# Score and product passes on 64x128 tiles beside PV sums on 64x32 tiles in a fused attention and gated MLP kernel

## Chip, cores and metric

The kernel runs on one core of a Trainium2 chip, as one program. The metric is the device time of one execution in microseconds (us). TensorE (PE in the profile) multiplies matrices on an array of 128 rows by 128 columns, which can be addressed in tiles: a form such as `64*32` in the profile means a tile of 64 rows (of the contraction) and 32 columns (of the output's partitions). ScalarE is ACT, VectorE DVE, GpSimd POOL, and SyncE (SP) issues most DMAs.

## The reference

What is computed, with x of shape 1 x 2048 x 448 in bf16, 16 heads of 28 columns and a hidden layer of 1792:

```
xn  = layernorm(x)
q, k, v = split(xn @ wqkv)                       # 16 heads, 28 columns each
p   = softmax(q @ k^T * 28**-0.5)                # 2048 x 2048 for each head
s   = (p @ v, heads side by side) @ wo
g   = silu(gelu(xn @ w1 + b1) @ w2 + b2)
out = x + s * g
```

## The kernel before

The heads are taken in 4 groups of 4 (`G`), the queries in 4 chunks of 512 (`C`): 16 blocks. A block has 64 score tiles `m`: 16 key tiles of 128 keys times 4 heads, each 128 keys x 512 queries in one bank of the PSUM ring of 8 banks (`ring`). Scores stand with the keys on the partitions. ScalarE takes the exponential of two banks (at times three) at once into `P` (L1790); some score tiles ("late" ones) go instead through a bit trick on VectorE (`p_apass`, L2075) into spare pieces of other buffers (`x_sb`, `w2`, `kT`, `vaug`, `h` and so on), which is why the inputs of L2341 have so many names in the profile. The PV sums (`t_pv`, L2341) multiply these with `vaug` or `vs`: 28 value columns of a head, a column for the denominator and three of zeros, so 32 columns a head; the 4 heads of a group go into the 4 column strips of one accumulator bank. Between these run the products: queries, keys and values of the later groups (L136, L1517), the hidden layer (L136 with `w1`), the second layer (L136 with `w2`), the output projection (L136 with `wo`). VectorE takes most of their banks out again. In the tables these lines carry the names that the profile gives (`w<-h` for a product of `h` with `w2`, for instance).

The order of all of this is made before anything runs: the class `_Kernel` is a list scheduler in Python. Processes (`p_scores`, `p_exps`, `p_pv`, `p_f1` and others) yield tasks with an engine, reads, writes and a planned duration; `run` picks the next task by its earliest start and its priority and puts it at the end of its engine's queue, with the semaphore waits that `deps` finds. The durations are constants in the text (`STEP` = 0.216 for a pass); how many matmuls a task issues does not enter.

TensorE works in one of four modes. `full` uses the whole array, `col` uses tiles of 128*32 for products and PV sums, `row` uses tiles of 32*128 for up to four scores of different heads (`t_score`, L1711). In the first 51 us and the last 38 us these take turns. In between, for most of blocks 0 to 14 (`HB0`, `HB1`), the mode is `half`: the array's rows are two halves, 0 to 63 and 64 to 127, and each pass uses one half `h`. A score tile (`t_half`, L1734) takes the two heads of its half, with the queries in `qp` laid out so that the rows of the other head are zero. A product splits its contraction of 128 into two halves, which one after another add into the same bank (`product`, lines 514 to 527). A PV pass adds the 64 keys of its half for four tiles (`t_pv` with `h`). A half pass, before, is four matmuls on four tiles of 64*32, at `tile_position` (64h, 0), (64h, 32), (64h, 64), (64h, 96): for scores and products these are four strips of the same output, for PV sums the four heads. Planner and TensorE can so keep both halves busy with passes of any kind. The planner counts a price (`SWITCH` = 0.1) where the mode changes, and none inside `half`; between halves it waits where the same bank is written by the other half (lines 249 to 252).

Filler passes (`filler`, `p_busy`) multiply zeros into the accumulator where TensorE would be idle for long; there are few. `p_qn` (L1448) writes four strips for four chunks and keeps its own tiles.

## Time and profile before

| what | value |
|---|---|
| median of 2 runs | 430.15 us (429.64 to 430.67) |
| the profiled execution | 428.93 us, its span 426.7 us |
| TensorE matmuls | 408.6 us busy (96%), 12,221 instructions |
| TensorE weight loads | 208.1 us busy (49%), 12,221 instructions |
| ScalarE | 403.8 us busy (95%), 435 instructions |
| VectorE | 331.0 us busy (78%), 568 instructions |
| GpSimd | 224.8 us busy (53%), 250 instructions |
| mean granted TensorE clock | 0.999 |
| the costliest matmul groups | L1734 64\*32 scores 200.7 us (x3460); L136 `w<-h` 99.0 (x1736); L2341 `P`, `vaug` 93.3 (x971); L136 `xnT`, `w` 88.4 (x1664) |

How to read it: busy time is the union of an engine's instructions. Matmuls overlap one another, and each ends some 0.17 us after it has taken in its last column, so a busy TensorE is not one at its peak; the time from the start of one matmul to the start of the next on the same tile is the better measure. In a timeline row stand the start in us, the length of the row, the engine, the line, the operation, what is written and read, the tile (rows\*columns), the shape of the moving operand, the count, and in brackets the idle time before and what ended it. In a row of the windows stand the window, its length, and then busy time and count for matmuls, weight loads, VectorE, ScalarE and GpSimd (for one line: matmuls and weight loads alone), the granted clock, the DMA share and GB/s. In a row of the waits stand who waited, for whom, the total, the number of times and the longest.

### The profile page before, as it was taken

Reading aid. Unit: us, or ns where it says so; the run is one execution under the profiler, and the core shown is the slowest. Engines: PE = TensorE matmul, PEld = TensorE weight load, DVE = VectorE, ACT = ScalarE, POOL = GpSimd, SP = SyncE. Lnnn points to the kernel's source line nnn. Section 1 sums busy time; section 2 is a strip of 40 time slices with the busy share of each in tenths; the row PEclk is TensorE's granted clock in tenths of the full one; section 3 lists DMA queues with packets and bytes.
Section 4 is the critical chain, followed back from the end, with each engine's and each line's share of the span. In section 5 each row is a group of like instructions: output and inputs, shape, how many; then the busy total and the mean of one; then the engine's idle time right before and its main releaser. Section 6 shows DMA issues by size and latency. Waiting matters only on the chain.

```text
span 426.7 us, 27054 instructions
## 1 busy us (share of the span) xinstructions
PE 408.6 (96%) x12221; PEld 208.1 (49%) x12221; DVE 331.0 (78%) x568; ACT 403.8 (95%) x435; POOL 224.8 (53%) x250
## 2 busy tenths in 40 slices
PE   6999999989999999999999999999999999999996
PEld 5443245554444444444445645445655555544563
DVE  8958987946888779996876426448698979778985
ACT  6999999989999999999999899889999999999794
POOL 7496376526376535348444723517735435765040
PEclk9999999999999999999999999999999999999999
DMA  8702201011001000101141330501010101011056
GB/s 251 274 3 47 33 4 42 21 28 36 22 4 38 17 24 17 39 7 28 25 148 42 59 73 7 113 4 32 17 30 17 30 18 29 6 47 29 3 102 144
DMA packets 21233, 20.41 MB, mean 48 GB/s; under 512 B 9709, under 2 KB 17693, under 8 KB 21086
## 3 DMA queue, kind: packets, MB, share of 16 engines
q1 hardware_dynamic: 18990, 15.10, 12.6%
q0 software_dynamic: 1152, 3.02, 4.2%
q8 instruction: 95, 1.56, 1.5%
q10 hardware_dynamic: 976, 0.57, 0.5%
q14 instruction: 20, 0.16, 0.1%
HBM read 12.54 MB, written 2.88 MB: 36 GB/s over the span
## 4 chain that ended last, share of the span: by engine, by line
PE 86%; ACT 6%; issue 4%; DVE 2%; POOL 1%; ACTq 0%; POOLq 0%; DVEq 0%
PE ring L136 31%; PE ring L1734 25%; PE ring L2341 23%; ACT P L1790 5%; PE ring L1711 3%; PE ring L1517 2%; PE ring L1307 1%; ACT h L1790 1%; POOL x_sb L2142 0%; ACT xnT L1790 0%; PE ring L1238 0%; DVE h L2500 0%; PE ring L1259 0%; DVE h L2477 0%; DVE qT L1294 0%
## 5 line engine op out<-in xcount | busy, mean ns | idle before, releaser
L1790 ACT ACTIVATE P<-ring 128x1024 bf16<-128x1024 f32 (+1 forms) x241 | 236.1, 1112 | 7.1 <-PE ring L1734 2.0
L1734 PE MATMUL ring<-qp,kT 64*32 64x512 bf16 x3460 | 200.7, 381 | 2.3 <-issue 0.9
L1734 PEld LDWEIGHTS ring<-qp,kT 64*32 64x32 bf16 x3460 | 59.0, 89 | 87.8 <-ACT P L1790 35.2
L136 PE MATMUL ring<-w,h 64*32 64x448 bf16 (+1 forms) x1736 | 99.0, 350 | 0.0
L2341 PE MATMUL ring<-P,vaug 64*32 64x512 bf16 (+3 forms) x971 | 93.3, 361 | 1.1 <-PE ring L1734 0.7
L1790 ACT ACTIVATE h<-ring 128x1024 bf16<-128x1024 f32 (+1 forms) x92 | 88.5, 1135 | 1.8 <-PE ring L1734 0.9
L136 PE MATMUL ring<-xnT,w 64*32 64x512 bf16 x1664 | 88.4, 377 | 1.5 <-issue 1.4
L2075 DVE TENSOR_SCALAR vaug<-ring 128x512 uint16<-128x512 f32 x68 | 45.1, 684 | 14.1 <-PE ring L1734 6.2
L136 PEld LDWEIGHTS ring<-w,h 64*32 64x32 bf16 (+1 forms) x1736 | 41.9, 92 | 16.2 <-issue 1.8
L1790 ACT ACTIVATE xnT<-ring 128x1024 bf16<-128x1024 f32 (+2 forms) x44 | 45.5, 1088 | 1.7 <-PE ring L2341 1.0
L2341 PE MATMUL ring<-h,vaug 64*32 64x512 bf16 (+2 forms) x405 | 44.7, 376 | 0.2
L136 PEld LDWEIGHTS ring<-xnT,w 64*32 64x32 bf16 x1664 | 33.4, 91 | 21.4 <-PE ring L136 3.9
L2448 POOL TENSOR_TENSOR qT<-x_sb,E_sb 128x512 bf16<-128x512 f32 x15 | 17.5, 1165 | 49.6 <-DMA x_sb<-recs 39.7
L2437 POOL TENSOR_TENSOR rc<-rs,mone 128x16 f32<-128x16 bf16 x11 | 32.9, 2988 | 19.3 <-DMA rs<-E_sb 14.5
L2075 DVE TENSOR_SCALAR w<-ring 128x512 uint16<-128x512 f32 x52 | 34.8, 686 | 7.4 <-PE ring L1734 3.5
L2075 DVE TENSOR_SCALAR x_sb<-ring 128x512 uint16<-128x512 f32 x48 | 32.0, 686 | 9.3 <-PE ring L1734 7.6
L2341 PEld LDWEIGHTS ring<-P,vaug 64*32 64x32 bf16 (+1 forms) x971 | 28.0, 92 | 10.9 <-issue 1.6
L136 PE MATMUL ring<-xnT,wq 64*32 64x512 bf16 (+1 forms) x372 | 30.4, 379 | 1.2 <-issue 1.0
L136 PE MATMUL ring<-xnT,wk 64*32 64x512 bf16 (+1 forms) x360 | 28.2, 379 | 0.2 <-ACT P L1790 0.2
L2341 PE MATMUL ring<-x_sb,vs 64*32 64x512 bf16 (+1 forms) x284 | 27.4, 377 | 0.3 <-POOL x_sb L2142 0.3
L2341 PE MATMUL ring<-xnT,vaug 64*32 64x512 bf16 (+2 forms) x208 | 26.8, 341 | 0.4 <-issue 0.4
L1538 DVE TENSOR_SCALAR h<-ring,b1c 128x512 bf16<-128x512 f32 x32 | 23.8, 744 | 2.7 <-PE ring L136 2.0
(251 smaller groups left out, 764.7 us busy)
## 6 DMA issues: line engine op xcount, KB each, us to landing
x_sb<-recs SPq DMA_DIRECT2D x60, 64.0 KB, 2.2
qp<-qT SPq DMA_DIRECT2D x60, 32.0 KB, 2.2
w<-in_B_w_dram SPq DMA_DIRECT2D x1, 1568.0 KB, 8.6
w<-in_B_w_dram SPq DMA_DIRECT2D x1, 1344.0 KB, 8.5
x_sb<-in_A_x_dram SPq DMA_DIRECT2D x2, 448.0 KB, 5.7
out_dram<-in_A_x_dram SPq DMA_DIRECT2D x2, 448.0 KB, 10.5
out_dram<-h POOLq DMA_DIRECT2D x4, 224.0 KB, 5.7
out_dram<-h SPq DMA_DIRECT2D x7, 112.0 KB, 1.7
```

What stands on the lines that cost most here:

```text
L136: ins = eng.matmul(out[q:q + 32, :], w[:, q:q + 32], x, tile_position=(r0, q), start=start, stop=stop, skip_group_check=True)
L1307: yield _Task(PE, lambda eng: eng.matmul(bank[:, 0:256], K.ident[:, :], K.E_sb[:, 0, 0:256], start=True, stop=True), [K.b_id, K.b_pads], [ ...
L1517: ins = eng.matmul(bank[q:q + 32, 0:12 * DH], K.xnT[r0:r0 + n, k, t * 128 + q:t * 128 + q + 32], ap, tile_position=(r0, q), start=start, s ...
L1538: yield _Task(DVE, lambda eng: eng.tensor_scalar(dst, bank, K.b1c[:, ft:ft + 1], None, op0=ALU.add), [tok, K.b_b1c], wr, 0.69, 0.0, 2)
L1711: return eng.matmul(dst, K.kT[32 * j:32 * j + 32, g, t * 128:(t + 1) * 128], K.qT[32 * j:32 * j + 32, g, c * 512 + q0:c * 512 + q0 + nq], ...
L1734: ins = eng.matmul(bank[q:q + 32, col:col + nq], K.kT[sl, g, t * 128 + q:t * 128 + q + 32], K.qp[sl, b % 2, v, q0:q0 + nq], tile_position= ...
L1790: return eng.activation(reg[:, i0:i0 + n, :], src, ACTF.Exp, scale=SM_SCALE)
L2075: yield _Task(DVE, lambda eng: eng.tensor_scalar(K.part(u, k).bitcast(dt.uint16), K.like(u, bank), SM_SCALE * LOG2E * 128.0, (127.0 - EXP_ ...
L2341: return eng.matmul(acc[32 * j:32 * j + 32, q0:q0 + nq], w[sl], ap[sl, col:col + nq] if len(ap.shape) == 2 else ap[sl, col // 128:(col + n ...
L2437: yield _Task(POOL, lambda eng: eng.tensor_tensor(K.rc[:, :], K.rs[:, :], K.mone[:, 0:1].to_broadcast([128, 16]), ALU.pow), [K.b_srs, K.b_ ...
L2448: yield _Task(POOL, lambda eng: eng.tensor_tensor(dst, K.rb, E, ALU.mult), [K.b_rb, tE], [K.b_onT[g][c]], 1.15, 0.05, 1, port=True)
```

## The change

Three places issue the half passes of scores and products: `_mm`, which serves most products, the fillers and the second layer; `f` in `p_v1`, for the values of groups 1 to 3; and `f` in `t_half`, for scores. Each now issues one matmul on a tile of 64*128 at position (64h, 0) in place of the four. Without `h` (modes `col` and others) `_mm` and `p_v1` are as they were. PV sums and `p_qn` keep their tiles of 64*32. The planner's durations and priorities, and so every queue's order and all waits, stay.

```
 def _mm(eng, out, w, x, start, stop, h=None):
     ...
-    for q in range(0, 128, 32):
-        ins = eng.matmul(out[q:q + 32, :], w[:, q:q + 32], x, tile_position=(r0, q), start=start, stop=stop, skip_group_check=True)
+    n = 32 if h is None else 128
+    for q in range(0, 128, n):
+        ins = eng.matmul(out[q:q + n, :], w[:, q:q + n], x, tile_position=(r0, q), start=start, stop=stop, skip_group_check=True)
     return ins

 # p_v1
-            for q in range(0, 128, 32):
-                ins = eng.matmul(bank[q:q + 32, 0:12 * DH], K.xnT[r0:r0 + n, k, t * 128 + q:t * 128 + q + 32], ap, tile_position=(r0, q),
+            w = 32 if h is None else 128
+            for q in range(0, 128, w):
+                ins = eng.matmul(bank[q:q + w, 0:12 * DH], K.xnT[r0:r0 + n, k, t * 128 + q:t * 128 + q + w], ap, tile_position=(r0, q),
                                  start=start, stop=True, skip_group_check=True)

 # t_half
             for t, q0, nq, col in pc:
-                for q in range(0, 128, 32):
-                    ins = eng.matmul(bank[q:q + 32, col:col + nq], K.kT[sl, g, t * 128 + q:t * 128 + q + 32], K.qp[sl, b % 2, v, q0:q0 + nq],
-                                     tile_position=(64 * h, q), start=True, stop=True, skip_group_check=True)
+                ins = eng.matmul(bank[:, col:col + nq], K.kT[sl, g, t * 128:t * 128 + 128], K.qp[sl, b % 2, v, q0:q0 + nq],
+                                 tile_position=(64 * h, 0), start=True, stop=True, skip_group_check=True)
             return ins
```

## The prediction

> **What bounds the kernel now.** I read the page first, its busy shares, its clock row and its chain, then the windows for the stretch that the change touches, then the timeline row by row.

> ```profile
> span 426.7 us, 27054 instructions
> ...
> PE 408.6 (96%) x12221; PEld 208.1 (49%) x12221; DVE 331.0 (78%) x568; ACT 403.8 (95%) x435; POOL 224.8 (53%) x250
> ...
> PEclk9999999999999999999999999999999999999999
> ...
> PE 86%; ACT 6%; issue 4%; DVE 2%; POOL 1%; ACTq 0%; POOLq 0%; DVEq 0%
> ```

> TensorE and ScalarE are both nearly full, at full clock, and 86% of the chain that ended last is matmuls. ScalarE makes the exponentials from the scores; anything that slows TensorE by more than a few per cent makes ScalarE wait, and nothing hides it. The passes in two row halves (tile 64*32) fill one stretch, from the first row of L1734 in that form to the first score row back in 32*128:

> ```profile
> 51.10:389.40 338.30, 329.98 (x10665) 168.80 (x10662) 257.04 (x403) 329.16 (x343) 182.91 (x175) 1.00 0.14 33
> ...
> 51.10:389.40 338.30, 194.34 (x2552) 64.13 (x2552) 1.00 0.14 33
> ...
> L1734 PE MATMUL ring<-qp,kT 64*32 64x512 bf16 x3460 | 200.7, 381 | 2.3 <-issue 0.9 <-ACT P L1790 0.8 <-DVE wq L2075 0.4
> ...
> PEld ring L1734 <- ACT P L1790: 35.2, 123, 1.0
> ```

> The first row is all engines (matmuls, weight loads, VectorE, ScalarE, GpSimd), the second L2341, the PV sums, alone: 2,552 of 10,665 matmuls. A pass is four of them, one per 32 columns. The last row shows the slack there is: score loads wait 35.2 us for exponentials, in 123 places. Inside this stretch the two halves run side by side whatever they compute:

> ```profile
> 108.03 0.39 PE L2341 MATMUL ring<-h,vaug 64*32 64x512 bf16 x4
> 108.06 0.39 PE L1734 MATMUL ring<-qp,kT 64*32 64x512 bf16 x4
> 108.25 0.38 PE L2341 MATMUL ring<-h,vaug 64*32 64x512 bf16 x1
> 108.25 0.38 PE L2341 MATMUL ring<-P,vaug 64*32 64x512 bf16 x3
> 108.28 0.39 PE L136 MATMUL ring<-xnT,wq 64*32 64x512 bf16 x4
> 108.46 0.39 PE L2341 MATMUL ring<-P,vaug 64*32 64x512 bf16 x4
> 108.50 0.39 PE L136 MATMUL ring<-xnT,w 64*32 64x512 bf16 x4
> 108.71 0.40 PE L1734 MATMUL ring<-qp,kT 64*32 64x512 bf16 x8
> ```

> A PV pass in one half starts at 108.03, a score pass in the other 0.03 us later, and so on: three PV passes beside a score and two product passes, six passes in 108.71 - 108.03 = 0.68 us. A half takes a new pass each 0.216 us or so (108.03, 108.25, 108.46). All of them have one shape, so nothing separates them.

> **What a change of shape costs.** The change gives scores and products the shape 64*128 and leaves the PV sums at 64*32. That pair is nowhere in this trace, but other changes of shape are:

> ```profile
> 15.63 0.39 PE L1711 MATMUL ring<-qT,kT 32*128 32x512 bf16 x2 [0.18 <-DVE xnT L1152]
> 15.96 0.39 PE L1307 MATMUL ring<-E_sb,ident 128*128 128x256 bf16 x2
> 16.28 0.62 PE L136 MATMUL ring<-xnT,wk 128*32 128x512 bf16 x8
> ...
> 20.44 0.39 PE L1711 MATMUL ring<-qT,kT 32*128 32x512 bf16 x2
> 20.76 0.61 PE L2341 MATMUL ring<-P,vaug 128*32 128x512 bf16 x8
> 21.31 0.39 PE L1711 MATMUL ring<-qT,kT 32*128 32x512 bf16 x2
> ...
> 52.02 0.41 PE L1734 MATMUL ring<-qp,kT 64*32 64x512 bf16 x8
> 52.36 0.62 PE L2341 MATMUL ring<-h,vaug 128*32 128x512 bf16 x8
> ```

> From 20.44 to 20.76 is 0.32 us where the same shape would have followed after 0.216: 0.10 us is lost. It is the same when only the rows change (52.02: two passes, the second 0.01 later, then 0.33 to 52.36) and when only the columns change (15.96: two matmuls of 256 columns, 0.107 each, so streaming ends at 16.17, and the next starts at 16.28). I did this for all 111 neighbours of different shape in the timeline: none starts less than 0.090 us after the stream before it should have ended, 92 lie between 0.090 and 0.107 (the others waited for something else), the median is 0.099. For 64*32 to 64*128 I take 0.098, with 0.090 and 0.106 as ends; its nearest row is the change of columns alone, at 15.96.

> Does one half's change stop the other half? Two rows near the end say so:

> ```profile
> 393.33 0.75 PE L136 MATMUL ring<-w,h 64*32 64x448 bf16 x12
> ...
> 394.01 0.12 PEld L1711 LDWEIGHTS ring<-qT,kT 32*128 32x128 bf16 x6 [0.37 <-issue]
> 394.01 0.40 PE L1711 MATMUL ring<-qT,kT 32*128 32x256 bf16 x6
> ```

> By the kernel's list the three product passes at 393.33 are all in the lower half (rows 64 to 127), and the first score matmul behind them is head row 1, rows 32 to 63, which nobody uses. It still starts only at 394.01: the third pass starts at 393.33 + 0.75 - 0.36 = 393.72 and streams 0.19 us, to 393.91, and then the usual 0.09 to 0.10 passes; the view names no other releaser ("issue"). So a change waits for both halves. [...]

> **The change, part by part.** Removed: three of four matmuls and loads of each score and product pass. L136, L1517 and L1734 have 8,112 matmuls of shape 64*32, 2,028 passes, so 6,084 go and about 6,137 of 12,221 stay. That gains next to nothing: four matmuls of a pass start 3 ns apart and stream together, and the half is busy 0.216 us either way. Walking the list of passes with one clock for each half, 0.216 us per 512 columns and a few ns of issue, gives 304.4 us for the stretch with four matmuls a pass and 302.7 with one. The stretch took 338.3, so 33.9 us of it are waits for banks and other engines.

> Added: the changes of shape. No pass moves in any queue and no DMA is touched. The stretch holds 642 PV-like passes (2,552 matmuls of L2341, of which 8 are in another shape, and 24 of one small line that keeps 64*32) between 1,994 score, product and filler passes. In the list they fall into 552 runs of PV passes and 556 runs of the others; 488 of the PV runs are a single pass, and 543 of 552 lie in one half alone, so the other half stands idle meanwhile. With three short returns to 128*32 there are 1,111 changes. A run lasts as long as its fuller half, then both drain:

> - PV runs: 632 passes in the fuller halves x 0.2158 = 136.4 us.
> - Score and product runs: 1,295 passes in the fuller halves (831 of 512 columns, 369 of 448, 86 of 336, 9 fillers) = 262.9 us.
> - 1,111 changes x 0.098 = 108.9 us.
> - Stagger of the halves inside runs and the three short returns: 5.6 us.

> Together 513.8 us (504.9 with 0.090 a change, 522.7 with 0.106). The six passes from 108.03 show it small: six runs of one pass, 6 x (0.216 + 0.098) = 1.88 us in place of 0.68.

> Of the 33.9 us of waits most should go: score loads no longer wait for exponentials, since a pair of scores now comes each 1.6 us or so and its exponential takes about 1.1. What is left are turns of one bank from half to half, where TensorE waits for its own pass in the other half; between two such turns there is now a change or two more. The bounds are 0 and 33.9; I take 6, near the lower end, since TensorE takes 1.5 times as long for the same order. Behind each drain stands the rest of TensorE's queue; the first to wait for it is ScalarE for scores, then VectorE for products and late scores, both with time to spare then.

> A weight load of 128 columns in place of 32 could show after a change, where nothing covers it. The drain at 20.44 to 20.76 leads into 32-column loads, the one at 393.33 to 394.01 into 128-column loads, and both are 0.09 to 0.10, so I add nothing; the case is a rival below.

> Sum: the profiled execution took 428.93 us, 2.2 outside its span of 426.7. 428.93 - 338.3 + 513.8 + 6 = 610.4. The median of the runs shown, 430.15, lies 1.2 higher. I say **610 us**.

> **The rivals.**

> - Each half drains by itself, and the other goes on. The list then has 659 changes within a half, and the walk gives 352.9 us. Some to all of the 33.9 us of waits stay, since ScalarE is again close: 428.93 - 338.3 + 352.9 + 17 = 460 (443 to 477). For it: the halves are separate rows. Against: the row at 394.01.
> - Not slower: between 64*32 and 64*128 there is no change at all for the hardware, since the rows stay. One place decides, the start of a PV pass in one half while a score pass streams in the other: if it may start, nothing is added and the walk falls by 1.7, to 427. Against: 15.96 to 16.28, where the columns alone change. With even a zero price but shapes that exclude each other the walk is 405.0, so the time 502.
> - The longer loads show: behind each of the 556 changes into 64*128 a whole load of 92 ns (the row of L1711 below) stands after the drain. 556 x 0.092 = 51: 661. Against: that row is of 128-column loads too, and the drains into them are no longer than others. [...]
> - Two 64*128 passes cannot stream side by side. Then score and product runs take the sum of their halves, 404.7 in place of 259.6 of pure stream, 145 more: 755. Against: four row tiles of 128 columns start together in the last row below, and are done in 0.41 us, as two are in 0.39 at 20.44.

> ```profile
> L1734 PEld LDWEIGHTS ring<-qp,kT 64*32 64x32 bf16 x3460 | 59.0, 89 | 87.8 <-ACT P L1790 35.2 <-ACT h L1790 13.0 <-ACT xnT L1790 5.8
> ...
> L1711 PEld LDWEIGHTS ring<-qT,kT 32*128 32x128 bf16 x287 | 8.4, 92 | 18.1 <-ACT P L1790 5.2 <-issue 4.8 <-ACT h L1790 2.3
> ...
> 31.21 0.41 PE L1711 MATMUL ring<-qT,kT 32*128 32x512 bf16 x4
> ```

> **How the numbers follow.** Drain of both halves at each change: 0.80. Each half by itself: 0.07. No drain: 0.05. Drain at no price but no overlap: 0.03. Longer loads that show: 0.03. No two passes side by side: 0.02. The likeliest case's own range is 428.93 - 338.3 + 504.9 = 595 to 428.93 - 338.3 + 522.7 + 33.9 = 647; I reach a little beyond both ends, 580 to 660, for what the walk leaves out. Only the case without a drain lies within 2% of before, about what a measurement of this kernel can tell: same 0.04, faster 0.01, slower 0.95.

> **What would show it.** Right: about 6,140 matmuls; in the timeline, rows of L2341 and of score lines no longer overlap and start 0.31 us after one another where single; ScalarE's share falls from 95% to about 66% (403.8 of 608) with idle time put down to L1734's successor; clock still full. The stretch of the two halves is near 520 us and the rest of the span, 88 us, as before. Wrong: PV and score rows that start within 0.05 us of one another; then the time is under 480. Or a gap after a change well off 0.10 us: each 0.01 is 11 us.

## The result, and the profile after

The changed kernel takes 640.38 us (638.01 to 642.74, two runs) against 430.15: 1.489 times the time before, interval 1.464 to 1.514. Four further runs gave 638.63 us (636.62 to 641.75) beside 430.01 for the kernel before, ratio 1.486 (1.479 to 1.494). The profiled execution took 642.74 us, its span 640.5.

The page of the kernel after, from its first, second and fourth part, and the ScalarE group of the fifth (busy time, mean ns, then idle time before and what ended it):

```profile
span 640.5 us, 14886 instructions
...
PE 628.9 (98%) x6137; PEld 204.9 (32%) x6137; DVE 335.7 (52%) x568; ACT 428.6 (67%) x435; POOL 223.5 (35%) x250
...
PEclk9999999899999999999999998559996699999999
...
PE 93%; DVE 2%; ACT 2%; issue 1%; DMA 0%; ACTq 0%; DVEq 0%
...
L1791 ACT ACTIVATE P<-ring 128x1024 bf16<-128x1024 f32 (+1 forms) x241 | 247.1, 1053 | 122.8 <-PE ring L1735 99.8
```

Matmuls fell to 6,137, and yet TensorE is 98% busy and 93% of the chain. ScalarE does the same 435 instructions, but at 67% of the span: it now waits 99.8 us for score rows alone in this group. The clock row, all nines before, has three dents.

The timeline of the kernel after, matmuls only, near the same time as the passes quoted before from 108.03 (an earlier place in the order):

```profile
107.76 0.40 PE L2342 MATMUL ring<-h,vaug 64*32 64x512 bf16 x4
108.09 0.31 PE L1519 MATMUL ring<-wv,xnT 64*128 64x336 bf16 x1
108.09 0.39 PE L1735 MATMUL ring<-qp,kT 64*128 64x512 bf16 x1
108.24 0.30 PE L1519 MATMUL ring<-wv,xnT 64*128 64x336 bf16 x1
108.38 0.38 PE L1735 MATMUL ring<-qp,kT 64*128 64x512 bf16 x1
108.69 0.40 PE L2342 MATMUL ring<-w,vaug 64*32 64x512 bf16 x4
109.02 0.31 PE L1519 MATMUL ring<-wv,xnT 64*128 64x336 bf16 x1
```

Two passes on 64\*128 tiles start together at 108.09, one in each half, so these do overlap. The PV pass does not: the four matmuls of L2342 start alone at 108.69, 0.31 us after the score row at 108.38 (0.216 of streaming and 0.09 more), and the next shape starts 0.33 us after that. Between 108.69 and 109.02 one half of the rows does nothing. The six passes quoted before stand at 138.5 to 140.65 here: the score pass joins the scores ahead of it, and the other five start runs of their own, at 139.03, 139.36, 139.67, 140.00 and 140.32, with the next run at 140.65; that is 0.32 us a run. The view of the waits, TensorE's loads, gives such time no releaser ("issue"; total, times, longest):

```profile
PEld ring L2342 <- issue: 140.2, 456, 0.8
...
PEld ring L137 <- issue: 86.8, 348, 0.4
```

Where the clock row dents, the windows of the same execution (window, length, busy time and count of matmuls, loads, VectorE, ScalarE, GpSimd, then granted clock, DMA share, GB/s) are:

```profile
51.00:395.70 344.70, 343.71 (x3011) 107.34 (x3011) 173.53 (x263) 239.51 (x232) 123.13 (x122) 1.00 0.09 23
395.70:429.90 34.20, 34.20 (x170) 7.42 (x166) 9.20 (x14) 12.91 (x13) 4.96 (x3) 0.50 0.03 10
429.90:484.50 54.60, 54.60 (x474) 16.92 (x470) 26.15 (x41) 33.70 (x33) 17.47 (x15) 1.00 0.04 11
484.50:508.40 23.90, 23.90 (x130) 5.99 (x130) 6.88 (x12) 9.05 (x8) 6.18 (x6) 0.50 0.01 1
508.40:604.00 95.60, 95.60 (x846) 29.26 (x847) 46.89 (x75) 59.71 (x59) 31.90 (x31) 1.00 0.07 16
```

Two windows, 58.1 us together, ran at half clock with TensorE busy in all of their length; a third of 3.4 us at 119.3 lies inside the first row, whose mean still rounds to 1.00.

The account: the stretch in halves went from 338.3 to 552.2 us (50.98 to 603.18), what follows it stayed at 37.3, what precedes it at 51. The 552.2 are 513.8 that the walk through the order gave, 5.6 because a change of shape cost 0.103 us in the mean at full clock rather than 0.098 (1,111 changes), 27.6 for the half clock, and 5.2 that is left for waits and all else. (The mean of 0.103 holds 14 changes that waited for something else; without them it is 0.101, and some 2 us move from the second term to the last.) The 27.6 is worked out: 61.4 us were spent at half clock, and the walk gives 33.8 us for the same passes at full clock.

### The profile page after: what moved, and what is told of

Read it like the earlier page. It is cut to its first block, busy times and chain, and to the rows that moved or that the text cites. A ratio compares the mean times of both kernels' runs of the same rounds, so it can differ in the third digit from the quotient of the medians.

```text
span 640.5 us, 14886 instructions
## 1 busy us (share of the span) xinstructions
PE 628.9 (98%) x6137; PEld 204.9 (32%) x6137; DVE 335.7 (52%) x568; ACT 428.6 (67%) x435; POOL 223.5 (35%) x250
## 4 chain that ended last, share of the span: by engine, by line
PE 93%; DVE 2%; ACT 2%; issue 1%; DMA 0%; ACTq 0%; DVEq 0%
PE ring L2342 34%; PE ring L137 34%; PE ring L1735 20%; PE ring L1519 3%; PE ring L1713 2%; ACT P L1791 2%; DMA x_sb<-in_A_x_dram 0%; DVE st L1069 0%; DVE w L2394 0%; DVE h L2501 0%; PE ring L1449 0%; PE ring L1260 0%; DVE h L2480 0%; DVE h L2478 0%; DVE qT L1295 0%
## 5 line engine op out<-in xcount | busy, mean ns | idle before, releaser
L1791 ACT ACTIVATE P<-ring 128x1024 bf16<-128x1024 f32 (+1 forms) x241 | 247.1, 1053 | 122.8 <-PE ring L1735 99.8
L1735 PE MATMUL ring<-qp,kT 64*128 64x512 bf16 x865 | 219.9, 398 | 0.7 <-DVE vaug L2076 0.4
L137 PE MATMUL ring<-w,h 64*128 64x448 bf16 (+1 forms) x476 | 125.5, 381 | 0.0
L2342 PE MATMUL ring<-P,vaug 64*32 64x512 bf16 (+3 forms) x971 | 106.9, 381 | 0.0
L137 PE MATMUL ring<-xnT,w 64*128 64x512 bf16 x416 | 95.2, 380 | 0.1
L1735 PEld LDWEIGHTS ring<-qp,kT 64*128 64x128 bf16 x865 | 50.7, 95 | 70.9 <-issue 43.9
L137 PEld LDWEIGHTS ring<-w,h 64*128 64x128 bf16 (+1 forms) x476 | 35.4, 98 | 60.2 <-issue 46.8
L2342 PE MATMUL ring<-h,vaug 64*32 64x512 bf16 (+2 forms) x405 | 48.5, 384 | 0.1
L2342 PEld LDWEIGHTS ring<-P,vaug 64*32 64x32 bf16 (+1 forms) x971 | 26.7, 91 | 64.1 <-issue 40.9
L137 PEld LDWEIGHTS ring<-xnT,w 64*128 64x128 bf16 x416 | 28.1, 94 | 38.9 <-issue 19.5
L137 PE MATMUL ring<-xnT,wq 64*128 64x512 bf16 (+1 forms) x141 | 31.9, 383 | 0.2 <-DVE w L2076 0.2
L2342 PE MATMUL ring<-xnT,vaug 64*32 64x512 bf16 (+2 forms) x208 | 29.9, 385 | 0.0
L137 PE MATMUL ring<-xnT,wk 128*32 128x512 bf16 (+1 forms) x150 | 29.5, 382 | 0.2 <-ACT P L1791 0.2
L2342 PE MATMUL ring<-x_sb,vs 64*32 64x512 bf16 (+1 forms) x284 | 28.9, 397 | 0.0
```

Of the source, the lines that this page charges most:

```text
L137: ins = eng.matmul(out[q:q + n, :], w[:, q:q + n], x, tile_position=(r0, q), start=start, stop=stop, skip_group_check=True)
L1735: ins = eng.matmul(bank[:, col:col + nq], K.kT[sl, g, t * 128:t * 128 + 128], K.qp[sl, b % 2, v, q0:q0 + nq], tile_position=(64 * h, 0), s ...
L1791: return eng.activation(reg[:, i0:i0 + n, :], src, ACTF.Exp, scale=SM_SCALE)
L2342: return eng.matmul(acc[32 * j:32 * j + 32, q0:q0 + nq], w[sl], ap[sl, col:col + nq] if len(ap.shape) == 2 else ap[sl, col // 128:(col + n ...
```

## The experiments

Theory A: a change between 64\*32 and 64\*128 drains both halves, at about 0.10 us, and while passes of one shape run none of the other can; the time follows the order of shapes. Theory C, the rival: a pass on a 64\*128 tile costs more by itself, so the loss (209 us for 2,028 passes) follows the number of such passes. A third question is the clock.

**after_again** is the kernel after once more, to size the half clock.

> The changed kernel unaltered, in several executions. Theory A: the 28 us by which it is over the forecast are the time at the half clock (61 us of it in the profiled execution, where streaming takes twice as long). Then executions differ in their clock, and the time goes with it: about 0.44 us more per us at half clock, so some 613 us + 0.44 x (time at half clock), 638 to 643 at 0.958 to 0.95. Rival B: the 28 us come from waits or a higher price of a change of shape; then the time does not go with the clock.

Measured: 638.63 us as above, and the profile has its dents at 119 to 143 and 542 to 573: the first begins where the short one did and lasts longer, the other is at a new place. The pairs of granted clock and span, with the first two runs, are 0.950 and 640.5, 0.958 and 635.9, 0.957 and 637.4, 0.960 and 635.8, 0.955 and 639.7, 0.962 and 634.5. Time at half clock is 2 x (1 - clock) x span, so 48 to 64 us; from the last pair to the first, 15.8 us more of it make the span 6.0 longer, about 0.4 us for each. So the loss to the clock is real, near 20 to 28 us in every run, and not tied to one place in the order.

**scores_only** and **products_only** do one part of the change each.

```
 # scores_only: the edit in t_half alone; _mm and p_v1 as before
 # products_only: the edits in _mm and p_v1 alone; t_half as before
```

> Scores on 64x128, products and PV sums on four tiles of 64x32. Theory A (each change of shape drains both halves, 0.103 us): the list has 891 changes, and the walk with two clocks gives 450 us for the stretch of the halves in place of 524; with 84 us outside it and some 8 of waits 540 to 550 us at full clock, up to 20 more where the clock falls. Rival C (each 64x128 pass costs something for itself, its longer load above all): 864 of 1,994 passes have the new shape, so 430 + 0.43 x 210 = 520 us. The two lie close here; products_only tells them apart.

> Products on 64x128, scores and PV sums on four tiles of 64x32. Theory A: fewer passes have the new shape than in the changed kernel, but there are more changes, 1,199 against 1,117, since scores now stand against products; the walk gives 538 us, so about 625 to 632 us at full clock and 640 to 665 with 30 to 60 us at half clock: no faster than the changed kernel. Rival C (a price for each 64x128 pass): 1,130 of 1,994 passes, 430 + 0.57 x 210 = 549 us.

Measured, one run each: scores_only 542.2 us, clock 0.998, 865 passes changed and 891 changes of shape: inside A's 540 to 550, and C's 520 is out. products_only 692.03 us, with 1,163 passes changed and 1,199 changes of shape: slower than the whole change, which C (549) excludes. It is also slower than A's figure, which allowed at most 60 us at half clock. Its windows show why:

```profile
51.00:477.00 426.00, 424.22 (x5706) 132.16 (x5698) 209.12 (x320) 286.02 (x278) 145.31 (x140) 1.00 0.09 21
477.00:613.60 136.60, 136.60 (x994) 27.76 (x990) 36.69 (x58) 44.64 (x42) 23.68 (x23) 0.50 0.03 6
```

136.6 us at half clock; with 0.45 us lost in each (27.6 of 61.4), 61 us, which leaves 631, inside A's 625 to 632 for full clock. A's mechanism holds, and my size for the clock was a miss.

**micro** leaves out the whole of the computation and runs streams of matmuls, with 50 of 128\*128 ahead of each.

```
A  100 passes of 64*128, both halves in turn, 512 columns
B  the same with four of 64*32 a pass
C  60 passes: 64*128 in the upper half, four of 64*32 in the lower, in turn
D  60 passes: the same pair, both in the upper half
E  as C, 100 passes of 128 columns
F  250 of 64*128 in the upper half alone
G  250 of 32*128 in one quarter of the rows alone
H  as D, 200 passes
```

> Not the reference's computation: x is copied out, and TensorE runs streams of matmuls on a part of wqkv, each after 50 matmuls of 128x128. A: 100 passes of 64x128 in both halves in turn. B: the same with four of 64x32. C: 64x128 in the upper half and four of 64x32 in the lower, in turn, 512 columns. D: the same, both in the upper half. E: as C with 128 columns. F: 250 passes of 64x128 in one half, nothing changes. G: 250 of 32x128 in one row tile. H: 200 as D. Theory A (a change drains both halves, about 0.10 us whatever streams): a pass starts 0.108 us after the one before in A and B, 0.31 in C and D, 0.155 in E. Rival D (each half drains by itself): C as A, 0.108 us, and D 0.31. Rival C (long loads show): A slower than B. On the clock: if it is held by how much of the array works (F half, G a quarter, H about a third, all without a gap of over 0.2 us), it falls in G and perhaps in H, not in F; if it is held by TensorE having something to do at all, it stays full in all three.

Measured in its timeline, matmuls only, the streams A, B and the starts of C and D:

```profile
16.92 10.96 PE L32 MATMUL ps<-w 64*128 64x512 bf16 x100
...
38.71 10.99 PE L37 MATMUL ps<-w 64*32 64x512 bf16 x400
...
60.53 0.39 PE L32 MATMUL ps<-w 64*128 64x512 bf16 x1
60.84 0.40 PE L37 MATMUL ps<-w 64*32 64x512 bf16 x4
61.17 0.39 PE L32 MATMUL ps<-w 64*128 64x512 bf16 x1
61.49 0.40 PE L37 MATMUL ps<-w 64*32 64x512 bf16 x4
...
102.16 0.39 PE L32 MATMUL ps<-w 64*128 64x512 bf16 x1
102.48 0.40 PE L37 MATMUL ps<-w 64*32 64x512 bf16 x4
```

One shape throughout costs 0.11 us a pass, wide or four strips alike (10.96 and 10.99 us for 100), so wide passes run side by side and are not dearer. The two shapes in turn cost 0.32 us a pass (60.53, 60.84, 61.17, 61.49), three times as much, though they lie in different rows. D, in the same rows, is 0.32 too (102.16, 102.48), so a change in one half drains the other. E takes 0.16 us a pass for streams of 128 columns, some 0.05 us each: the price of about 0.10 does not hang on the length. The streams C and D agree and set the price.

The clock in the same run, by windows around the stream C, for F, and for G:

```profile
60.50:66.20 5.70, 5.70 (x46) 1.72 (x45) 0.00 (x0) 0.00 (x0) 1.00 0.00 0
66.30:89.30 23.00, 22.87 (x109) 4.52 (x107) 0.00 (x0) 0.00 (x0) 0.50 0.00 1
177.30:231.20 53.90, 53.90 (x251) 23.38 (x250) 0.00 (x0) 0.00 (x0) 1.00 0.00 1
242.20:247.10 4.90, 4.90 (x24) 2.15 (x24) 0.00 (x0) 0.00 (x0) 1.00 0.00 0
247.20:344.00 96.80, 96.80 (x228) 33.22 (x226) 0.00 (x0) 0.00 (x0) 0.50 0.00 0
```

C fell to half clock 5.7 us after its start. F, half of the array without a change, kept full clock for 53.9 us. G, a quarter of the array without any change or pause, fell after 4.9 us and stayed down. D, E and H fell as well, 4.4 to 5.5 us after their start. TensorE was busy all the time; what differs is how much of the array took in columns: 0.50 in F, 0.25 in G, and in C one half at a time for 0.216 of each 0.325 us, so 0.33.

**uniform** takes the other way to one shape: the PV sums in halves become one matmul on a 64\*128 tile too. It leaves out three quarters of these PV sums (the four heads' weights side by side meet the scores of one head only), so its time shows the shapes, with the same passes, order and waits.

```
 # the change, and in t_pv with h, for the first of four heads alone:
+ eng.matmul(acc[:, q0:q0 + nq], w4[sl], <scores>, tile_position=(64 * h, 0), ...)   # w4: vaug or vs of four heads, 128 columns
```

> Every half pass is one matmul of 64x128, PV passes too: of a PV pass's four products only the one of the first head is computed, against the value columns of all four heads, so three quarters of the PV sums are left out. The passes, their order and the time that each streams are as before, and but for six passes nothing changes shape. Theory A (the loss is in the changes of shape): the walk gives 303 us for the stretch in place of 304, so 426 to 431 us, same as before, and the clock stays full, since both halves work. Rival C (64x128 costs something for itself: its load, or two of them not side by side): slower than before, toward 640.

Measured: 421.24 us (420.96 to 421.93) beside 431.31, ratio 0.977 (0.974 to 0.979). With every half pass on a 64\*128 tile nothing of the loss is left, and the clock is 1.0: the wide tile is harmless, mixing is not. It came 5 us below A's 426 to 431: that it beats before by 10 us I had not expected; the last section comes back to it.

**runs30, runs5** and **runs3** keep the order and give the wide tile only to passes that stand in a run of at least 30, 5 or 3 passes without a PV pass; the rest keep four of 64\*32.

```
+LONG = 30        # 5, 3
 # _mm, p_v1, t_half:
+n = 128 if <run of this task has LONG tasks or more> else 32
 for q in range(0, 128, n): ...
```

> Order as before; 64x128 only in score and product passes that stand in a run of 30 or more of them without a PV pass between: 266 passes in 3 runs, the longest in the GELU stage. Theory A: a handful of changes more, the walk 310.2 against 308.8 us, less what 800 fewer matmuls save: 427 to 432 us, same as before. If 64x128 passes themselves were the loss (Rival C), 13% of them would cost some 28 us.

> As the one before, with runs of 5 or more: 1,158 of 1,994 passes at 64x128, but only 243 changes in place of 1,117. Theory A: the walk gives 351 us against 309, of which the 29.5 us of waits in the old order cover a part: 453 to 472 us, clock full. Rival C (by passes): 430 + 0.58 x 210 = 552 us.

> As before, with runs of 3 or more: 1,660 passes at 64x128 and 548 changes. Theory A: the walk gives 411 us, waits mostly covered: 505 to 525 us at full clock. Rival C: 430 + 0.83 x 210 = 604 us.

Measured:

| kernel | passes on 64\*128 (matmuls in the trace) | changes of shape | time |
|---|---|---|---|
| runs30 | 266 | 6, around 3 runs | 425.33 us (beside 428.84), ratio 0.993 (0.991 to 0.996) |
| runs5 | 1,171 | 243 | 448.57 us, one run |
| runs3 | 1,684 | 548 | 506.38 us, one run |
| scores_only | 865 | 891 | 542.2 us, one run |
| the change | 2,028 | 1,111 | 638.63 us |

More passes do not cost more: runs5 and runs3 have more wide passes than scores_only and are faster. C's figures, 552 and 604, are both out. runs5 came 4 us below A's range and runs30 2 us below its own, runs3 inside it. By the 2% that the prediction took for what one measurement can tell, runs30 is the same as the kernel before; over 10 and 13 runs its interval lies 0.4 to 0.9% below it and does not reach 1, so a small gain is likely real. Of the kernels that compute everything it is the fastest.

**priced** lets the planner know: a change of shape inside `half` costs `SWITCH`, as a change of mode does, and drains. **priced32** runs that new order on the old tiles of 64\*32, so that no change of shape is left in it.

```
+ if t.mode != self.pe_mode or t.mode == "half" and t.shape != self.pe_shape:   # shape=1 for PV tasks
 # priced: with the change; priced32: _mm, p_v1, t_half as before
```

> The changed tiles, with the planner told that a change between PV sums and the other half passes costs 0.1 us and drains both halves, so that it makes another order. Its list has 325 changes in place of 1,117; the walk gives 436 us in place of 524, and the planner's own dates, with its waits, some 457 for the stretch. Theory A: 535 to 565 us, faster than the changed kernel by 70 us or more, with the clock full or nearly. Rival E (the number of changes does not matter, the tiles do): 630 to 640 as in the changed kernel.

> The order of the kernel with the priced planner, on the old tiles, four of 64x32 a pass: what that order costs where nothing changes shape. The walk gives 386 us against 436. Theory A: 40 to 60 us less than with the new tiles, 485 to 525 us. Rival E: about 430 us, since the tiles are the old ones.

Measured: priced 551.99 us (two runs), ratio 1.280 (1.276 to 1.284), with 325 changes in place of 1,111, in its range. priced32 539.92 us (one run), above the 485 to 525 expected: a miss. With its changes of shape the new order takes only 12 us more than without them (priced32 also lost some us to 10.3 us at half clock, from 327.5); most of the loss of priced is the order. The waits of priced32 show ScalarE behind PV sums and score loads behind ScalarE:

```profile
ACT P L1793 <- PE ring L2344: 61.5, 18, 9.1
PEld ring L1737 <- ACT P L1793: 48.3, 106, 1.3
```

In before, ScalarE's idle time ahead of the same group is 7.1 us in all (its page, fifth part):

```profile
L1790 ACT ACTIVATE P<-ring 128x1024 bf16<-128x1024 f32 (+1 forms) x241 | 236.1, 1112 | 7.1 <-PE ring L1734 2.0
```

The longest of these waits, in the timeline of priced32:

```profile
335.34 6.84 PE L136 MATMUL ring<-w,h 64*32 64x448 bf16 x132
...
342.01 0.60 PE L2344 MATMUL ring<-P,vaug 64*32 64x512 bf16 x8
...
342.53 2.37 ACT L1793 ACTIVATE P<-ring 128x1024 bf16<-128x1024 f32 x2 [9.07 <-PE ring L2344]
```

An exponential may overwrite a part of `P` only when the PV passes that read it are done (`p_exps` waits for `pv_done`). With passes of one shape collected, TensorE here runs 33 product passes from 335.34, and the PV passes that free `P` come at 342.01. So the planner pays for fewer changes with exponentials that wait for PV sums. Better priorities may do better; that was not tried.

**split** tests the gain of uniform from the other side: more instructions, no change of shape. Each score pass and most product passes of before become eight matmuls of half the columns. Theory F: the rate at which instructions reach TensorE bounds it; theory G: the number of instructions is free.

```
+ for a in range(0, nq, 256):
      for q in range(0, 128, 32): eng.matmul(<columns a to a + 256 of the same>)
```

> The kernel before with each score pass and most product passes of the two halves issued as eight matmuls of 64x32 with half the columns each, in place of four: some 7,500 matmuls and loads more, no other shape, the same columns streamed in the same order. Theory F (few matmuls are faster because TensorE at times runs out of instructions: the kernel before has nine pauses of 0.47 to 1.41 us that no semaphore explains, the one with one matmul a pass has one): more such pauses, 445 us or more. Theory G (the 10 us that one matmul a pass saves come from something else, such as PV passes that are lighter): 428 to 433 us.

Measured: 631.22 us (627.62 to 634.83), ratio 1.471 (1.432 to 1.509): G is out, and F is far stronger than I expected. Page and waits of split, and its timeline, matmuls only, across one pause:

```profile
span 625.5 us, 42078 instructions
...
PE 446.1 (71%) x19733; PEld 330.6 (53%) x19733; DVE 329.5 (53%) x568; ACT 418.1 (67%) x435; POOL 223.4 (36%) x250
...
q8 instruction: 154, 2.52, 1.7%
```

```profile
PEld ring L139 <- issue: 121.3, 93, 3.9
PE ring L139 <- issue: 96.5, 69, 3.5
```

```profile
200.18 0.28 PE L139 MATMUL ring<-xnT,w 64*32 64x256 bf16 x3
...
201.56 0.29 PE L139 MATMUL ring<-xnT,w 64*32 64x256 bf16 x4 [1.02 <-issue]
```

TensorE stops after three matmuls of a group of four and goes on at 201.56, 1.02 us after its last row ended; no semaphore lies between. There are 131 such pauses, in which no matmul or load starts for over 0.45 us, 201 us together; split is 202 us longer than before. Each of them ends 1.2 to 1.7 us after a packet of the instruction queue (q8 above) has landed, though the packets come 3.74 us apart in the median, so the pauses are tied to these packets.

## Why the prediction was right, and where it was not

The forecast was 610, in the range 580 to 660; measured were 640.38 and 638.63, some 30 above it.

- **A change drains both halves: right.** The timeline at 108.38 to 109.02, and the micro streams C and D, show it directly; the rivals of a drain in one half (460), of none (427) and of an exclusion without a price (502) are out. The small example in the prediction read the order wrongly: its six passes make five runs, not six, in 1.62 us (139.03 to 140.65).
- **Its price: nearly right.** The 552 changes into 64\*32 have a median of 0.102 and the 552 back 0.106, smallest 0.092 and 0.095; the mean at full clock is 0.103 (0.101 without the 14 that waited), inside 0.090 to 0.106. Against 0.098 that is 5.6 us, or 3.3.
- **The walk, 513.8: right** as far as the sum can show it, with 6,137 matmuls as forecast and the rest of the span, 51.0 + 37.3, as before.
- **Waits, 6: right, as far as a remainder can show it.** 5.2 to 7.5 are left for them, and of 1,141 gaps at changes of shape at full clock only 14 exceed 0.12 us, together 2.5 us. ScalarE's share, 67%, was forecast at 66, though its busy time rose as well, from 403.8 to 428.6.
- **"Clock still full": wrong, and this is the step that failed.** The stretch came out at 552.2 in place of near 520, and 27.6 of that is the half clock. The prediction carried the full clock of before over to the kernel after, without a reason. But a PV pass that stands alone leaves half of the array idle and the drain all of it: where single passes take turns the share is 0.216 x 0.5 / 0.32 = 0.34, below the 0.363 behind which the clock fell. What the sum should have had is a question by stage: where a run of single changes makes the working share of the array a third, does the clock hold? The trace of before could not answer (from 7 us to the end of its work none of its windows has less than 0.47), and both forms of its answer belonged into the range. That 640 lies in the range all the same is luck: the room at its upper end was meant for up to 33.9 us of waits, and the clock, which nobody had counted, filled it.
- **The longer loads (661) and no two passes side by side (755): out.** The total comes within 21 us of the first, but the changes into 64\*128 cost 0.106 against 0.102 the other way, nothing like 0.092 more; and the rows at 108.09 start together.
- The removal of 6,084 matmuls I took as worth 1.7 us. In uniform, with 7,992 fewer matmuls, it is worth about 10 where nothing else is in the way. In the change this gain is hidden, since TensorE waits for drains (1,111 of 0.103 us), not for instructions: in its stretch no pause of over 0.45 us at full clock is without a semaphore.

## What to carry to other kernels

Before giving some passes a tile of another shape, count how often the shape changes in TensorE's order, over both halves, not how many passes get it: each change cost 0.103 us here in the mean, and a run of one shape kept the other out. 266 passes in 3 long runs gained 0.7%, 2,028 in 556 runs cost 49%. And where a change leaves part of the array idle, put the half clock into the range, even when TensorE's busy share stays near 100% (98% here): count the columns in windows of 3.413 us, and look where the share of the array comes near the 0.363 or less behind which the clock fell in these runs.

## What the runs showed of the hardware that was not expected

**In these runs the clock followed how much of the array worked, not whether TensorE was busy.** The row of the kernel after from 395.70 has 34.20 of 34.20 us busy at 0.50. F, on half of the array, kept full clock for 53.9 us; G, on a quarter, fell after 4.9 us while streaming without a pause (4.90 of 4.90 us busy). Here is how a pass looks at half clock in the kernel after, at 0.5 us a pass and change:

```profile
398.13 0.62 PE L2342 MATMUL ring<-xnT,vaug 64*32 64x512 bf16 x4
398.68 0.55 PE L137 MATMUL ring<-w,h 64*128 64x448 bf16 x1
399.16 0.61 PE L2342 MATMUL ring<-P,vaug 64*32 64x512 bf16 x4
399.71 0.55 PE L137 MATMUL ring<-w,h 64*128 64x448 bf16 x1
```

**In these runs instructions arrived at a bounded rate, and the kernel before is close to it.** The third part of each page counts packets of the instruction queue q8, of 16 KB each: 154 in split (above), and in before, after and uniform in turn:

```profile
q8 instruction: 95, 1.56, 1.5%
```

```profile
q8 instruction: 48, 0.79, 0.5%
```

```profile
span 419.7 us, 11070 instructions
...
PE 405.9 (97%) x4229; PEld 182.3 (43%) x4229; DVE 327.3 (78%) x568; ACT 401.7 (96%) x435; POOL 224.5 (53%) x250
...
q8 instruction: 33, 0.54, 0.5%
```

Before has 2 x 12,221 matmuls and loads on 95 packets, 257 to a packet; the same count gives 256 in split, in after and in uniform. These packets follow each other at a median of 3.74 us in split and 3.86 us in before, never closer than 3.27; in after it is 14.5 and in uniform 15.3. In the stretch of before TensorE gets through 21,327 matmuls and loads in 338.3 us, 63 a microsecond; in the same stretch of split (51 to 588) it is 36,270 in 537, 68. Before has 9 pauses of over 0.45 us without a semaphore in its stretch, 8.25 us together (the first at 86.6, the last at 386.6), runs30 has 7 with 4.3 us, uniform none in its stretch (one behind it). These pauses too end 1.2 to 1.6 us after a packet of q8 has landed, all nine in before and all seven in runs30. So the 10 us by which uniform is faster and the 3.5 of runs30 fit the pauses that went; this much is argued from the counts, while split shows that the limit is there.
